# Sparse attention and two MLPs on one core: the weight conversions beside attention cut into smaller ScalarE steps, the high part copied on VectorE, and a new table of stage offsets

## The chip, the cores and the metric

One core of one Trainium2 chip runs the whole program in one launch. The metric is the device time of an execution in microseconds; of several executions the median counts. The time before is 1178.81 us, the median of three runs from 1178.59 to 1180.55.

## What is computed

Cut to what matters, the reference is (all in float32):

```python
scores = (q @ k.T) / 8                      # q, k, v: 4 batches x 8 heads x 576 rows x 64
keep = scores >= scores.max(-1) - tau       # tau 0.02
attn = where(keep, exp(scores - scores.max(-1)), 0)
x = (attn / (attn.sum(-1) + 1e-9)) @ v      # put side by side by head: 2304 x 512
h = x @ moe_w_in                            # 512 -> 2048
x = (maximum(h, 0) + alpha * minimum(h, 0)) @ moe_w_out    # 2048 -> 512
h = x @ moe2_w_in
out = where(h > 0, h, exp(minimum(h, 0)) - 1) @ moe2_w_out
```

The weights of the MLPs and alpha arrive as float64 and are read by the kernel as pairs of 32-bit words.

## The kernel before

**Attention** comes first. It works on 16 units, a unit being a batch and two heads of it, and on 9 jobs in each unit: four blocks of 128 query rows for each of the two heads, and one last job that holds the 64 rows left over of both heads. Job `j` has `j % 9` as its place in the unit; the last job of a unit has place 8. A job goes through these stages (class `Job`):

- `scores`: TensorE matmuls of `qt` with `kt` into a PSUM tile `ps`, of which there are three;
- `top`: VectorE takes the negated maximum of a row (a TENSOR_REDUCE into `st`); `limit`: GpSimd makes the threshold from it (`st<-st,tau_sb`);
- `exp`: ScalarE writes `e` from `ps`; `mask`: VectorE zeroes what lies under the threshold and sums (`e<-ps,st,e`); with it the tile `ps` is free;
- `raise_sum` on GpSimd and `invert` on VectorE give the reciprocal of the sums, for two heads at a time; `normalise`: GpSimd multiplies `e` by it (`e<-e,st`);
- `turn` and `turn_last`: TensorE transposes `e` into a PSUM bank `pst`; `keep` and `keep_last`: ScalarE copies the bank to `pt`;
- after four or five jobs of a unit `values` multiplies `pt` with `vt` into such a bank (256 columns for a unit's first group, 320 for its second), and `finish` on ScalarE copies it to `xt`.

Beside this, `prep` and `keep_prep` transpose the next unit's `k` and `q`, on the same PSUM banks. There are two banks (`ps_t`, `bufs=2`), shared by `prep`, `turn`, `turn_last` and `values`: each of these waits until ScalarE has emptied the bank that was filled two before.

**The conversions.** The float64 weights are turned into a high and a low fp32 part, one piece of 128x512 at a time (`conversion`, line 118). Twenty pieces (those of the first ten blocks of the first MLP) are converted beside attention: ScalarE writes `x` (an absolute value, line 124) and `t` (the lower word, line 125), VectorE limits, shifts and joins bits (lines 128 to 139), GpSimd adds (line 140), ScalarE writes the high part `hi` (line 149, `w<-x` in the trace), VectorE writes the low part `lo` (line 153, `w<-x,w`). The function is a generator: each `yield` ends a step, and `beside` (line 546) runs one step at a time.

**The order** is written out. Everything on TensorE, VectorE, ScalarE and GpSimd goes through `Pinned` (line 81), so that each engine executes its instructions in the order in which the program issues them; all of these have line 87 in the profile. For attention, `attention` (line 390) puts every stage of every job into a list at the place `j + AT[stage]` (the table at line 386) and issues the list sorted by place. The steps of `beside` stand at 1.25 jobs from one another.

**The MLPs** follow: chunks of 512 tokens, `hidden` and `outer` for each of 16 blocks of the hidden layer, fed by TensorE without a break; `load_in` splits a chunk of the input into two parts, and the first chunk's loading is begun beside attention (line 549).

Of the kernel before, what the change touches and what calls it, by code (L numbers as in the profile page):

```python
# [12 lines left out]
AF = mybir.ActivationFunctionType  # L13
# [7 lines left out]
def sparse_attention_two_mlps(  # L21
# [29 lines left out]
    FIRST = 10  # L51
# [5 lines left out]
    stage = ctx.enter_context(tc.tile_pool(name="stage", bufs=2))  # L57
# [31 lines left out]
    pe, dve, act, pool = (Pinned(engine) for engine in (nc.tensor, nc.vector, nc.scalar, nc.gpsimd))  # L89
# [11 lines left out]
    def load_piece(i):  # L101
        if i >= len(pieces):
            return
        layer, f, part = pieces[i]
        src = ((moe_w_in, moe_w_out), (moe2_w_in, moe2_w_out))[layer][part]
        r = stage.tile([P, DM], I64, tag="raw", name="r64", bufs=3)
        if part == 0:
            nc.sync.dma_start(
                out=r.rearrange("p (k m) -> p k m", m=P),
                in_=src[:, f * P:(f + 1) * P].rearrange("(k p) m -> p k m", p=P))  # L110
        else:
            nc.sync.dma_start(out=r, in_=src[f * P:(f + 1) * P, :])
        both = r.bitcast(U32).rearrange("p (n t) -> p n t", t=2)
        staged[i] = both[:, :, 0], both[:, :, 1]
# [3 lines left out]
    def conversion(i):  # L118
        layer, f, part = pieces[i]
        lower, upper = staged.pop(i)  # L120
        x = stage.tile([P, DM], F32, tag="x", name="x", bufs=4)
        t = stage.tile([P, DM], U32, tag="t", name="t", bufs=3)
        bits = x.bitcast(U32)
        act.activation(out=x, in_=upper.bitcast(F32), func=AF.Abs)
        act.activation(out=t, in_=lower, func=AF.Copy, scale=2.0 ** -29)
        yield
        if layer == 0 and f < FIRST:
            dve.tensor_scalar(out=x, in0=x, scalar1=TOP, scalar2=BOTTOM, op0=ALU.min, op1=ALU.max)
            dve.tensor_scalar(out=bits, in0=bits, scalar1=5, scalar2=2,
                              op0=ALU.logical_shift_left, op1=ALU.logical_shift_right)  # L130
        else:
            dve.scalar_tensor_tensor(out=x, in0=x, scalar=TOP, in1=bottom.to_broadcast([P, DM]), op0=ALU.min,
                                     op1=ALU.max)
            dve.scalar_tensor_tensor(out=bits, in0=bits, scalar=5, in1=two.to_broadcast([P, DM]),
                                     op0=ALU.logical_shift_left, op1=ALU.logical_shift_right)
        if layer == 0 and f < FIRST:
            yield
        dve.scalar_tensor_tensor(out=bits, in0=upper, scalar=0xC0000000, in1=bits,
                                 op0=ALU.bitwise_and, op1=ALU.bitwise_or)
        pool.tensor_tensor(out=bits, in0=bits, in1=t, op=ALU.add)  # L140
        load_piece(i + 3)
        yield
        if layer == 1:
            hi, lo = t.bitcast(F32R), x.bitcast(F32R)
        else:
            if part == 0:
                wt[f] = new_block(f)
            hi, lo = wt[f][:, part, 0, :], wt[f][:, part, 1, :]
        act.activation(out=hi, in_=x, func=AF.Copy)
        if layer == 1:  # L150
            nc.sync.dma_start(out=w_d[f][:, part, 0, :], in_=t.bitcast(F32))
        yield
        dve.scalar_tensor_tensor(out=lo, in0=x, scalar=1.0, in1=hi.bitcast(F32), op0=ALU.mult, op1=ALU.subtract)
        if layer == 0:
            converted_parts.append(f)
        else:
            nc.sync.dma_start(out=w_d[f][:, part, 1, :], in_=x)

    def new_block(f):
        return wps[f >= FIRST].tile([P, 2, 2, DM], F32R, tag="w", name="w")  # L160
# [10 lines left out]
    def convert_step(limit):  # L171
        if not active and converted[0] < limit:
            active.append(conversion(converted[0]))
            converted[0] += 1
        if active and next(active[0], "end") == "end":
            active.pop()
# [61 lines left out]
    def prep(u, i):  # L238
        if i == 0:
            turned_in[u] = (raw.tile([P, 2, HS], F32, tag="kt", name="kt", bufs=2),  # L240
                            raw.tile([P, 2, S], F32, tag="qt", name="qt", bufs=2))
        ps = bank()
        h = i // 2
        kr, qr = raws[u][h]
        if i % 2 == 0:
            for t in range(HS // KB):
                pe.transpose(ps[:, t * KB:(t + 1) * KB], kr[:, t, :], ident[0:KB, 0:KB])
        else:
            for t in range(NKT):
                pe.transpose(ps[:, t * P:(t + 1) * P], qr[:, t, :], ident)  # L250
        if i == 0:
            for g in range(2):
                pe.transpose(ps[:, HS + g * TAIL:HS + (g + 1) * TAIL], raws[u][g][1][0:TAIL, NKT, :],
                             ident[0:TAIL, 0:TAIL])
        return ps
# [105 lines left out]
    def group_values(group):  # L361
        u, g = group
        vt, pt = vts[u % 2], pts.pop(group)
        n = 2 * P + g * TAIL
        ps = bank()
        for t in range(NKT):
            for h, own in halves():
                pe.matmul(out=ps[own, 0:n], lhsT=vt[:, t, own], rhs=pt[:, h * NKT + t, 0:n],
                          start=(t == 0), stop=False, skip_group_check=True)
        pe.matmul(out=ps[:, 0:n], lhsT=vt[:, NKT, :], rhs=pt[:, 2 * NKT, 0:n], start=False,  # L370
                  stop=True, skip_group_check=True)
        return ps

    def finish(group, ps):
        u, g = group
        if g == 0:
            xts[u] = raw.tile([P, S], F32, tag="xt", name="xt", bufs=2)
        n = 2 * P + g * TAIL
        act.activation(out=xts[u][:, 2 * g * P:2 * g * P + n], in_=ps[:, 0:n], func=AF.Copy)
        if g == 1:  # L380
            b, hp = units[u]
            nc.sync.dma_start(out=x_d[b][:, hp, :], in_=xts.pop(u))
            load_values(u + 2)


    AT = dict(scores=-3.09, prep=-2.6, keep_prep=-2.33, top=-2.24, limit=-2.07, exp=-2.01, mask=-0.67, raise_sum=-0.53,
              invert=0.13, beside=0.2, normalise=1.58, turn=2.01, keep=2.29, turn_last=2.97, keep_last=3.19,
              values=6.05, finish=6.46)

    def attention(beside):  # L390
        jobs = [Job(u, i, h) for u in range(len(units)) for i in range(NKT + 1) for h in range(2 if i < NKT else 1)]
        todo = []

        def put(at, what, *args):
            todo.append((at, len(todo), what, args))

        for j, job in enumerate(jobs):
            for stage in ("scores", "limit", "exp", "mask", "normalise", "turn", "keep"):
                put(j + AT[stage], getattr(job, stage))
            put(j + AT["top"], job.top, jobs[j - 1])  # L400
            if not (job.h or job.last):
                continue
            put(j + AT["raise_sum"], job.raise_sum)
            put(j + AT["invert"], job.invert)
            put(j + AT["turn_last"], job.turn_last, jobs[j - 1])
            put(j + AT["keep_last"], job.keep_last)
            if job.last or job.i == 1:
                held = []
                put(j + AT["values"], lambda g, held=held: held.append(group_values(g)), job.group)
                put(j + AT["finish"], lambda g, held=held: finish(g, *held), job.group)  # L410
            if not job.last and job.u + 1 < len(units):
                held = []
                put(j + AT["prep"], lambda u, i, held=held: held.append(prep(u, i)), job.u + 1, job.i)
                put(j + AT["keep_prep"], lambda u, i, held=held: keep_prep(u, i, *held), job.u + 1, job.i)
        for i in range(len(jobs) * 4 // 5):
            put(1.25 * i + AT["beside"], beside, i)
        for _, _, what, args in sorted(todo, key=lambda t: t[:2]):
            what(*args)

# [126 lines left out]
    def beside(i):  # L546
        if i > 4:
            convert_step(2 * FIRST)
        if i == 80 or i == 95:
            next(first_in, None)  # L550

    attention(beside)
    for _ in first_in:
        pass
# [36 lines left out]
```

## Time and profile before

| what | value |
|---|---|
| median of three runs | 1178.81 us |
| the profiled execution's own time | 1180.63 us |
| its span, first to last instruction | 1178.80 us |
| busy, share of the span | PE 96%, DVE 55%, ACT 44%, POOL 39% |
| granted TensorE clock | 0.999 of full speed |
| attention | from 4 us, when the first transposes start, to 367 us |
| the two MLPs | 367 us to the end |

The page names the engines PE (TensorE matmuls), PEld (TensorE weight loads, which run beside matmuls), DVE (VectorE), ACT (ScalarE), POOL (GpSimd) and SP (DMA issue). Names like `pst<-ident,e` say which tile an instruction writes and which it reads. An idle time is put down to the instruction whose end ended it. The profiled execution took 1.82 us longer than the median.

### The profile page before, as it was taken

The page shows a single profiled execution, that of the slowest core. Times are in us where ns is not written, and L with a number is a line of the kernel's source. Part 1 is how long each engine was busy: PE and PEld are TensorE (multiplying, and loading weights), DVE is VectorE, ACT ScalarE, POOL GpSimd, SP SyncE. Part 2 cuts the span into 40 slices and gives each one's busy share as a digit, 9 for nine tenths or more (in the row PEclk, how much of TensorE's full clock was granted, in tenths as well). Part 3 has the DMA queues.
Part 4 walks back from the last instruction along what each step waited for, and adds up shares of the span by engine and source line. Part 5 has one row for each costly group of instructions (what it writes and reads, how often), then busy time and mean ns, then how long its engine had stood idle before and what let it go on. Part 6 is the DMA issues. An engine that isn't in the chain of part 4 may idle for free.

```text
span 1178.8 us, 16654 instructions
## 1 busy us (share of the span) xinstructions
PE 1133.0 (96%) x5936; PEld 853.2 (72%) x5936; DVE 651.8 (55%) x1153; ACT 513.1 (44%) x988; POOL 458.7 (39%) x598
## 2 busy tenths in 40 slices
PE   7888999989898999999999999999999999999998
PEld 4555555555456888888888888978888888888887
DVE  5777876877774994686886862422232232232232
ACT  5787887887774442342342331222222222222222
POOL 3555655655553552443543542222222222222222
PEclk9999999999999999999999999999999999999999
DMA  6533543434212332345444424950010010010000
GB/s 146 141 101 98 148 102 89 120 88 112 59 38 75 103 94 98 126 155 184 162 152 169 162 79 145 369 185 1 3 70 1 1 72 1 1 54 1 1 36 19
DMA packets 126242, 110.67 MB, mean 94 GB/s; under 512 B 83920, under 2 KB 104400, under 8 KB 123600
## 3 DMA queue, kind: packets, MB, share of 16 engines
q1 hardware_dynamic: 126160, 109.61, 29.9%
q8 instruction: 47, 0.77, 0.3%
q14 instruction: 35, 0.29, 0.1%
HBM read 78.65 MB, written 30.93 MB: 93 GB/s over the span
## 4 chain that ended last, share of the span: by engine, by line
PE 67%; DMA 1%; ACT 0%; DVE 0%; issue 0%; SPq 0%; DVEq 0%; ACTq 0%
PE psa L87 34%; PE psh L87 32%; DMA y<-o 1%; PE pst L87 1%; DVE g L87 0%; DMA out_dram<-o 0%; ACT o L87 0%; ACT gh L87 0%; DVE o L87 0%; ACT xt L87 0%; DVE il L87 0%; ACT pt L87 0%; ACT g L87 0%; DMA x<-xt 0%; SPq L505 0%
## 5 line engine op out<-in xcount | busy, mean ns | idle before, releaser
L87 POOL TENSOR_TENSOR gl<-g,gh 128x512 fp32r<-128x512 f32 (+1 forms) x160 | 200.3, 1252 | 490.4 <-ACT gh L87 418.7
L87 PE MATMUL psh<-ih,w 128*128 128x512 f32 (+1 forms) x1280 | 385.9, 369 | 0.4 <-ACT ih L87 0.4
L87 PEld LDWEIGHTS psh<-ih,w 128*128 128x128 f32 x1280 | 233.7, 188 | 45.0 <-ACT ih L87 0.8
L87 ACT ACTIVATE gh<-g 128x512 fp32r<-128x512 f32 (+1 forms) x160 | 94.5, 591 | 330.8 <-DVE g L87 319.2
L87 PE MATMUL psh<-il,w 128*128 128x512 f32 (+1 forms) x640 | 236.8, 370 | 0.2 <-DVE il L87 0.2
L87 DVE TENSOR_SCALAR g<-g 128x512 f32<-128x512 f32 (+1 forms) x80 | 38.2, 477 | 253.9 <-ACT g L87 253.8
L87 PE MATMUL psa<-w,gh 128*128 128x512 f32 x576 | 148.7, 398 | 2.2 <-ACT gh L87 2.2
L87 DVE TENSOR_REDUCE st<-ps 128x1 f32<-128x576 f32 x144 | 108.6, 754 | 75.6 <-PE ps L87 75.1
L87 PE MATMUL psa<-gh,w 128*128 128x512 f32 (+1 forms) x640 | 147.8, 373 | 0.6 <-ACT gh L87 0.6
L87 PEld LDWEIGHTS psh<-il,w 128*128 128x128 f32 x640 | 120.2, 188 | 22.1 <-DVE il L87 0.5
L87 PEld LDWEIGHTS pst<-ident,e 128*128 128x128 f32 (+1 forms) x720 | 74.5, 137 | 80.0 <-issue 22.6
L87 PE MATMUL pst<-ident,e 128*128 128x128 f32 (+1 forms) x720 | 114.8, 285 | 17.1 <-POOL e L87 9.8
L87 PEld LDWEIGHTS psa<-gh,w 128*128 128x128 f32 x640 | 112.5, 188 | 23.5 <-ACT gh L87 0.8
L87 PEld LDWEIGHTS psa<-w,gh 128*128 128x128 f32 x576 | 107.6, 189 | 27.7 <-ACT gh L87 2.8
L87 DVE SCALAR_TENSOR_TENSOR e<-ps,st,e 128x576 f32<-128x576 f32 x144 | 115.9, 805 | 4.9 <-ACT e L87 4.0
L87 ACT ACTIVATE pt<-pst 128x512 f32<-128x512 f32 (+2 forms) x240 | 109.7, 464 | 15.8 <-PE pst L87 13.4
L87 ACT ACTIVATE g<-psh 128x512 f32<-128x512 f32 (+1 forms) x80 | 44.3, 553 | 165.3 <-PE psh L87 163.6
L87 POOL TENSOR_SCALAR e<-e,st 128x576 f32<-128x576 f32 x144 | 111.1, 772 | 9.7 <-DVE st L87 1.8
L87 PE MATMUL ps<-kt,qt 64*128 64x288 f32 (+1 forms) x640 | 111.4, 455 | 0.3 <-DVE e L87 0.3
L87 POOL TENSOR_TENSOR x<-x,t 128x512 uint32<-128x512 uint32 x64 | 82.3, 1287 | 72.3 <-DVE x L87 69.9
L87 ACT ACTIVATE e<-ps,st 128x576 f32<-128x576 f32 x144 | 106.6, 740 | 2.3 <-DVE st L87 2.3
L87 DVE SCALAR_TENSOR_TENSOR g<-psh,g 128x512 f32<-128x512 f32 (+1 forms) x160 | 102.1, 638 | 5.5
(45 smaller groups left out, 1142.7 us busy)
## 6 DMA issues: line engine op xcount, KB each, us to landing
r<-in_moe_w_in_dram SPq DMA_DIRECT2D x32, 512.0 KB, 3.7
r<-in_moe_w_out_dram SPq DMA_DIRECT2D x32, 512.0 KB, 3.5
w<-w SPq DMA_DIRECT2D x16, 1024.0 KB, 5.2
qr<-in_q_dram SPq DMA_DIRECT2D x64, 128.0 KB, 2.7
w<-t SPq DMA_DIRECT2D x32, 256.0 KB, 2.2
w<-x SPq DMA_DIRECT2D x32, 256.0 KB, 2.1
kr<-in_k_dram SPq DMA_DIRECT2D x64, 72.0 KB, 2.4
x<-xt SPq DMA_DIRECT2D x16, 288.0 KB, 2.5
```

What stands on the lines that cost most here:

```text
L87: return lambda *args, **named: tc.keep_in_program_order(made(*args, **named))
```

## The change

In the conversions beside attention (`beside_attention`: the first layer's first ten blocks) there is now a `yield` between the two ScalarE writes, the high part is copied by VectorE instead of ScalarE, and the low part follows it in the same step. A piece still takes five steps. The table of offsets is another one; a second table, `LATER`, moves some stages of the second head's jobs; the steps stand 1.3 jobs apart instead of 1.25, and the two steps of the first chunk's loading have other numbers.

```diff
+        beside_attention = layer == 0 and f < FIRST
         act.activation(out=x, in_=upper.bitcast(F32), func=AF.Abs)
+        if beside_attention:
+            yield
         act.activation(out=t, in_=lower, func=AF.Copy, scale=2.0 ** -29)
         yield
...
-        act.activation(out=hi, in_=x, func=AF.Copy)
+        if beside_attention:
+            dve.tensor_copy(out=hi, in_=x)
+        else:
+            act.activation(out=hi, in_=x, func=AF.Copy)
         if layer == 1:
             nc.sync.dma_start(out=w_d[f][:, part, 0, :], in_=t.bitcast(F32))
-        yield
+        if not beside_attention:
+            yield
         dve.scalar_tensor_tensor(out=lo, in0=x, scalar=1.0, in1=hi.bitcast(F32), op0=ALU.mult, op1=ALU.subtract)
...
-    AT = dict(scores=-3.09, prep=-2.6, keep_prep=-2.33, top=-2.24, limit=-2.07, exp=-2.01, mask=-0.67, raise_sum=-0.53,
-              invert=0.13, beside=0.2, normalise=1.58, turn=2.01, keep=2.29, turn_last=2.97, keep_last=3.19,
-              values=6.05, finish=6.46)
+    AT = dict(scores=-3.24, top=-2.4, limit=-2.37, prep=-2.29, exp=-2.11, keep_prep=-1.89, mask=-1.41, 
+                  raise_sum=-1.21, invert=-0.36, normalise=0.71, beside=1.96, turn=2.23, keep=2.5, turn_last=3.17, 
+                  keep_last=3.44, values=6.66, finish=6.97)
+    LATER = dict(normalise=-0.77, top=-0.23, scores=-0.19, keep=-0.02, turn=-0.0, mask=0.17, exp=0.29)
...
-                put(j + AT[stage], getattr(job, stage))
-            put(j + AT["top"], job.top, jobs[j - 1])
+                put(j + AT[stage] + job.h * LATER.get(stage, 0), getattr(job, stage))
+            put(j + AT["top"] + job.h * LATER["top"], job.top, jobs[j - 1])
...
-        for i in range(len(jobs) * 4 // 5):
-            put(1.25 * i + AT["beside"], beside, i)
+        for i in range(len(jobs) * 10 // 13):
+            put(1.3 * i + AT["beside"], beside, i)
...
-        if i == 80 or i == 95:
+        if i == 78 or i == 92:
             next(first_in, None)
```

What this does to the order is seen engine by engine. On TensorE the rows of the two programs are the same from first to last; none of its instructions has another place. On the other three engines the places at which they differ repeat from unit to unit; three are shown.

ScalarE at the end of the eighth unit, where `finish` (`xt<-pst 128x320`) empties the bank of the unit's second `values`. Before:

```order
L87 ACTIVATE qt<-pst,sc 128x512
L87 ACTIVATE e<-ps,st 128x576
L87 ACTIVATE pt<-pst 128x4x128
L87 ACTIVATE xt<-pst 128x320
L87 ACTIVATE e<-ps,st 128x576
L87 ACTIVATE pt<-pst 128x128
L87 ACTIVATE pt<-pst 128x4x128
L87 ACTIVATE w<-x 128x512
L87 ACTIVATE e<-ps,st 128x576
L87 ACTIVATE pt<-pst 128x4x128
```

The same place in the change:

```order
L87 ACTIVATE qt<-pst,sc 128x512
L87 ACTIVATE e<-ps,st 128x576
L87 ACTIVATE pt<-pst 128x4x128
L87 ACTIVATE e<-ps,st 128x576
L87 ACTIVATE xt<-pst 128x320
L87 ACTIVATE pt<-pst 128x128
L87 ACTIVATE pt<-pst 128x4x128
L87 ACTIVATE e<-ps,st 128x576
L87 ACTIVATE pt<-pst 128x4x128
L87 ACTIVATE x<-r_2072 128x512
```

The `exp` of the ninth unit's last job (job 80, the second `e<-ps,st` shown before, and the second in the change) has gone from behind the `finish` to ahead of it, and the conversion's `w<-x` is gone from ScalarE. Apart from conversions, this is the one difference on ScalarE, and it stands once in a unit.

GpSimd around the `normalise` (`e<-e,st`) of job 70, the last job but one of the eighth unit. Before:

```order
L87 TENSOR_SCALAR st<-st,tau_sb 128x1
L87 TENSOR_SCALAR st<-st 128x1
L87 TENSOR_SCALAR e<-e,st 128x576
L87 TENSOR_SCALAR st<-st,tau_sb 128x1
L87 TENSOR_TENSOR x<-x,t 128x512
L87 TENSOR_SCALAR e<-e,st 128x576
L87 TENSOR_SCALAR st<-st,tau_sb 128x1
L87 TENSOR_SCALAR st<-st 128x2
L87 TENSOR_SCALAR e<-e,st 128x576
```

The same place in the change:

```order
L87 TENSOR_SCALAR st<-st,tau_sb 128x1
L87 TENSOR_SCALAR e<-e,st 128x576
L87 TENSOR_SCALAR st<-st 128x1
L87 TENSOR_SCALAR e<-e,st 128x576
L87 TENSOR_SCALAR st<-st,tau_sb 128x1
L87 TENSOR_TENSOR x<-x,t 128x512
L87 TENSOR_SCALAR st<-st,tau_sb 128x1
L87 TENSOR_SCALAR e<-e,st 128x576
L87 TENSOR_SCALAR st<-st 128x2
L87 TENSOR_SCALAR st<-st,tau_sb 128x1
L87 TENSOR_SCALAR e<-e,st 128x576 x2
```

Before, `normalise` of job 70 (the second `e<-e,st`) stood behind `limit` of job 73 and a conversion's add (`x<-x,t`); in the change (there too the second `e<-e,st` shown) it stands ahead of `limit` of job 73 and of the add. Where two jobs are a pair, as jobs 72 and 73 in the last row, their two `normalise` now follow one another.

VectorE at the end of the ninth unit, around `top` (TENSOR_REDUCE) of job 81, the tenth unit's first, whose scores TensorE issues behind the eighth unit's second `values`. Before:

```order
L87 TENSOR_REDUCE st<-ps 128x1
L87 SCALAR_TENSOR_TENSOR e,st<-ps,st,e 128x576
L87 TENSOR_REDUCE st<-ps 128x1
L87 RECIPROCAL st<-st 128x2
L87 SCALAR_TENSOR_TENSOR e,st<-ps,st,e 128x576
L87 TENSOR_REDUCE st<-ps 128x1
L87 RECIPROCAL st<-st 128x1
L87 SCALAR_TENSOR_TENSOR w<-x,w 128x512
L87 SCALAR_TENSOR_TENSOR e,st<-ps,st,e 128x576
```

The same place in the change:

```order
L87 TENSOR_REDUCE st<-ps 128x1
L87 SCALAR_TENSOR_TENSOR e,st<-ps,st,e 128x576 x2
L87 TENSOR_REDUCE st<-ps 128x1
L87 RECIPROCAL st<-st 128x2
L87 CAST w<-x 128x512
L87 SCALAR_TENSOR_TENSOR w<-x,w 128x512
L87 TENSOR_REDUCE st<-ps 128x1
L87 SCALAR_TENSOR_TENSOR e,st<-ps,st,e 128x576
L87 RECIPROCAL st<-st 128x1
```

The `mask` of the unit's last job (job 80) has gone from behind `top` of job 81 to ahead of it; the reciprocal of a pair mostly stands one `mask` later; the copy of the high part (CAST `w<-x`) is new, with the low part right behind it.

## Rows read from the trace of the kernel before

**Rows 1.** Busy time by stage: stretch, busy us of each engine, clock, DMA share, GB/s.

```profile
20.00:350.00 330.00, 303.00 (x2053) 173.98 (x2054) 254.25 (x571) 258.19 (x528) 192.63 (x372) 1.00 0.40 104
350.00:367.00 17.00, 13.97 (x96) 7.66 (x95) 4.58 (x12) 7.42 (x18) 6.13 (x11) 1.00 0.05 18
367.00:1179.00 812.00, 804.32 (x3746) 664.23 (x3745) 386.76 (x554) 239.79 (x431) 257.23 (x204) 1.00 0.26 91
```

**Rows 2.** Waits in 20:367, TensorE's: who waited for whom, us in total, times, longest.

```profile
PEld pst L87 <- POOL e L87: 21.6, 31, 1.9
...
PEld pst L87 <- POOL st L87: 16.9, 37, 1.1
PE pst L87 <- ACT pt L87: 16.0, 30, 1.9
...
PE pst L87 <- POOL e L87: 9.8, 14, 1.4
```

**Rows 3.** The same view, the other engines.

```profile
POOL st L87 <- DVE st L87: 85.9, 68, 2.9
DVE st L87 <- PE ps L87: 64.5, 40, 3.0
ACT xt L87 <- PE pst L87: 57.7, 30, 2.4
```

**Rows 4.** Timeline, 184:196: start, us, engine, operation, [idle before <-releaser].

```profile
186.95 1.27 POOL L87 TENSOR_TENSOR x<-x,t 128x512 uint32<-128x512 uint32 x1 [0.81 <-ACT e L87]
...
188.21 0.74 POOL L87 TENSOR_SCALAR e<-e,st 128x576 f32<-128x576 f32 x1
...
189.00 0.66 PE L87 MATMUL pst<-ident,e 128*128 128x128 f32 x4 [1.39 <-POOL e L87]
```

**Rows 5.** Timeline, 301:314, ScalarE's conversions ahead of a bank.

```profile
303.37 0.66 ACT L87 ACTIVATE x<-r 128x512 f32<-128x512 f32 x1
...
304.49 0.61 ACT L87 ACTIVATE ih<-il 128x512 fp32r<-128x512 f32 x1
...
306.11 0.47 PE L87 MATMUL pst<-ident,kr 96*128 96x96 f32 x3 [1.87 <-ACT pt L87]
```

**Rows 6.** Timeline, 213:219, the same place of another unit, none between.

```profile
217.52 0.47 PE L87 MATMUL pst<-ident,kr 96*128 96x96 f32 x3 [0.23 <-ACT pt L87]
```

**Rows 7.** Timeline, 200:216, around a unit's second values.

```profile
201.95 3.11 PE L87 MATMUL pst<-pt,vt 128*64 128x320 f32 x18
...
205.10 0.44 ACT L87 ACTIVATE xt<-pst 128x320 f32<-128x320 f32 x1 [2.44 <-PE pst L87]
205.43 0.73 ACT L87 ACTIVATE e<-ps,st 128x576 f32<-128x576 f32 x1
...
205.79 0.76 DVE L87 TENSOR_REDUCE st<-ps 128x1 f32<-128x576 f32 x1 [2.50 <-PE ps L87]
```

**Rows 8.** Groups by form in 20:367: busy us, mean ns | idle before.

```profile
L87 ACT ACTIVATE e<-ps,st 128x576 f32<-128x576 f32 x141 | 104.4, 740 | 0.4 <-DVE st L87 0.4
...
L87 DVE SCALAR_TENSOR_TENSOR w<-x,w 128x512 fp32r<-128x512 f32 x20 | 15.7, 784 | 1.8 <-ACT w L87 1.8
...
L87 ACT ACTIVATE w<-x 128x512 fp32r<-128x512 f32 x20 | 12.5, 627 | 0.0
...
L87 DVE TENSOR_SCALAR x<-x 128x512 f32<-128x512 f32 x20 | 11.7, 586 | 1.3 <-ACT x L87 1.3
...
L87 DVE TENSOR_SCALAR x<-x 128x512 uint32<-128x512 uint32 x20 | 9.3, 466 | 0.7
```

**Rows 9.** Timeline, 184:196, a shift of VectorE's alone.

```profile
183.57 0.43 DVE L87 TENSOR_SCALAR x<-x 128x512 uint32<-128x512 uint32 x1
```

**Rows 10.** Timeline, 200:216, VectorE's conversions beside GpSimd's normalise.

```profile
208.03 1.01 DVE L87 SCALAR_TENSOR_TENSOR w<-x,w 128x512 fp32r<-128x512 f32 x1
...
212.57 0.74 POOL L87 TENSOR_SCALAR e<-e,st 128x576 f32<-128x576 f32 x1
...
212.72 1.33 DVE L87 TENSOR_SCALAR x<-x 128x512 f32<-128x512 f32 x2
```

More of the change, by code (lines that the diff above doesn't have):

```diff
@@ L123, in conversion @@
         bits = x.bitcast(U32)
+        beside_attention = layer == 0 and f < FIRST
         act.activation(out=x, in_=upper.bitcast(F32), func=AF.Abs)
+        if beside_attention:
+            yield
         act.activation(out=t, in_=lower, func=AF.Copy, scale=2.0 ** -29)
         yield
-        if layer == 0 and f < FIRST:
+        if beside_attention:
             dve.tensor_scalar(out=x, in0=x, scalar1=TOP, scalar2=BOTTOM, op0=ALU.min, op1=ALU.max)
@@ L135, in conversion @@
                                      op0=ALU.logical_shift_left, op1=ALU.logical_shift_right)
-        if layer == 0 and f < FIRST:
+        if beside_attention:
             yield
@@ L148, in conversion @@
             hi, lo = wt[f][:, part, 0, :], wt[f][:, part, 1, :]
-        act.activation(out=hi, in_=x, func=AF.Copy)
+        if beside_attention:
+            dve.tensor_copy(out=hi, in_=x)
+        else:
+            act.activation(out=hi, in_=x, func=AF.Copy)
         if layer == 1:
             nc.sync.dma_start(out=w_d[f][:, part, 0, :], in_=t.bitcast(F32))
-        yield
+        if not beside_attention:
+            yield
         dve.scalar_tensor_tensor(out=lo, in0=x, scalar=1.0, in1=hi.bitcast(F32), op0=ALU.mult, op1=ALU.subtract)
```

## The prediction, made before the changed kernel ran

> **What bounds the kernel now.** I read the busy times by stage first. From 367 us on TensorE is busy 804.3 of 812.0 us [rows 1], and the change touches nothing there: the MLPs will take what they take. Attention is where the time can move. From 20 to 350 us TensorE is busy 303.00 of 330 us, and in the last 17 us 13.97 [rows 1]. So it is idle 27.0 + 3.0 = 30.0 us between 20 and 367 us, and everything else in that stretch is its own work. Of the 330 us VectorE is busy 254.25, ScalarE 258.19 and GpSimd 192.63 [rows 1]; none of them is full.
>
> TensorE's order does not change at all, so the question is only which of its 30 us of waiting goes, and what waiting is new. The table of waits says whom it waits for: 16.0 us in 30 waits for ScalarE's copies to `pt`, that is for a PSUM bank to be emptied, and 9.8 us in 14 waits for GpSimd's `normalise` [rows 2]. Those two are 25.8 of the 30. The waits of the weight loads for GpSimd, 21.6 and 16.9 us [rows 2], run partly beside matmuls, so I take them only as an upper bound.
>
> The waits of the other engines show who is pushed and who pushes. VectorE waits 64.5 us in 40 waits for scores, and ScalarE 57.7 us in 30 waits for a bank that `values` fills [rows 3]. These are TensorE's long blocks: while TensorE spends 3.11 us on 18 matmuls of `values`, ScalarE stands 2.44 us in front of `finish`, the `exp` behind it runs only afterwards, and VectorE's next `top` comes after 2.50 us of idleness [rows 7]. Between two such blocks TensorE outruns ScalarE, and then waits for banks.
>
> **Part 1, GpSimd's order (gain).** One of the 14 waits can be followed: the conversion's add runs 1.27 us from 186.95, `normalise` runs behind it from 188.21, and TensorE, idle 1.39 us, starts its transposes at 189.00, when it ends [rows 4]. The `normalise` was queued behind a `limit` that needs a later job's `top`, and behind an add, though its own sums were long inverted. In the change the second `normalise` of a pair follows the first, one `limit` earlier than before, and the add comes behind. GpSimd's own work is the same. What is now queued behind two multiplications, 2 x 0.74 us [rows 4, 10], is the next `limit`. Between the reciprocal and the `mask` that needs this threshold VectorE has two `top` of 0.76 us [rows 7] and another `mask` to do, which are longer together, so I cost that delay at nothing; where an add stands between too (1.27 us [rows 4]), up to half a microsecond of VectorE's time is uncovered, mostly in front of `values`, where it is idle anyway. Of the 9.8 us I take all, and 0.2 more for single short waits of the same kind: **-10 us**. The bounds are 0, if something else releases TensorE just as late, and -14.0, all of the 30.0 us that are not ScalarE's 16.0 (the weight loads' 38.5 are more than there is to gain).
>
> **Part 2, ScalarE (gain).** ScalarE loses 20 copies of 627 ns, 12.5 us [rows 8]. The other two writes of a piece no longer stand together. And once in a unit an `exp` of 740 ns [rows 8] goes ahead of `finish`, into an idle time of 2.44 us [rows 7]: 16 x 0.74 = 11.8 us of ScalarE's work that no longer stand behind `values`, where TensorE next asks for banks. What such work costs TensorE is seen by comparing one place in two units. With three such writes in front, two of a conversion and one of the first chunk's loading (0.66 us the first, 0.61 the last) the transposes of the next keys waited 1.87 us [rows 5]; in a unit in which none of these came between, they waited 0.23 us [rows 6]. The 0.23 us belong to the ring of two banks and to the `exp` that stands between two copies, and stay. If all 30 waits shrank to that, 16.0 - 30 x 0.23 = 9.1 us would go. Single steps of 0.66 us remain in the queue, so I take **-8 us**. Bounds: 0, and -16.0.
>
> **Part 3, VectorE (loss).** VectorE gains 20 copies of 128x512 from SBUF to SBUF. The trace has no such copy on VectorE; the nearest rows are its one-source operations on the same tile, 586 and 466 ns on average [rows 8], one of them alone 0.43 us [rows 9]. Two of them took 1.33 us while GpSimd multiplied [rows 10]; less the 0.43 us of one that ran alone, the other took 0.90. I take 0.55 us, 11 us in all, with 0.43 and 0.90 as the ends (8.6 to 18 us). The low part, 784 ns on average [rows 8], follows at once, so that a block of 1.3 us stands ahead of a `top`, and behind it an `exp`, the `keep_last` behind that in ScalarE's queue, and a bank. Against it VectorE's `mask` of the unit's last job goes into the idle time of 2.50 us [rows 7], and VectorE has 64.5 us of idleness [rows 3], but only at `values`. That the reciprocal stands one `mask` later costs nothing, because `turn` asks for `normalise` more than a job later. I charge a quarter of the 11 us to the path: **+3 us**. The quarter is my choice; the bounds are 0 and, with the whole block as long as the rows show it can be, (0.90 + 1.01 - 0.78) x 20 = 22.6 us, where 1.01 us is a low part beside a multiplication [rows 10].
>
> **What costs nothing.** The longer offset of `values` moves none of its matmuls on TensorE. The steps are 1.3 jobs apart, so the twentieth piece ends some seven jobs later, still six jobs before the last one. The loads of the pieces, issued by SP at the joining of bits, and the loads behind `finish` shift by less than a job, and the DMA share is 0.40 before 350 us [rows 1]. The last 17 us have no conversions.
>
> **The sum**: -10 - 8 + 3 = -15 us. The profiled execution would go from 1180.63 to 1165.6; it lies 1.82 above the median of 1178.81, so against the median the time is **1164 us**.
>
> **The rivals.**
>
> - *The ring keeps the pace.* Only GpSimd's part comes true; ScalarE's relief is given back, because TensorE comes to the two banks earlier and waits there for the `exp` in between. For it speaks that a wait of 0.23 us stays without any conversion [rows 6]; against it the 1.87 us with them [rows 5]. -10 + 3: 1172.
> - *GpSimd and VectorE get into each other's way.* VectorE's shift took 0.43 us alone and its like 0.90 beside a multiplication [rows 9, 10], and with pairs of `normalise` GpSimd is busy 1.48 us at a stretch. A copy that meets a pair could be late by 0.47 + 0.74 = 1.2 us; with GpSimd busy 192.63 / 330 = 0.58 of the time [rows 1], that is 20 x 0.58 x 1.2 = 14 us of VectorE, of which I charge half, 7 us, less 1 that part 3 holds already: -15 + 6, which gives 1170. The Trainium skill's page "SBUF — State Buffer", section "Who interferes with whom", has a rule by which this must be so: a copy or a one-scalar operation of VectorE in a two-port mode and a GpSimd instruction exclude one another for a whole instruction. By that rule the move to VectorE is bought on the one engine that can be blocked; the 0.43 and 0.90 us agree with it.
> - *TensorE hardly waits any more.* The reliefs help one another, 25 of the 30 us go: 1154.
> - *No change.* Each wait that goes is followed by another of the same length, and the table, whose new offsets leave TensorE's order as it was, does nothing that counts: 1179, within 0.2% (2.4 us), about what a measurement of this kernel can tell from no change.
> - *Slower: VectorE's double step.* The copy and the low part, back to back ahead of a `top` that comes right behind `values`, hold up `top`, `exp`, the copies to `pt` and the banks. At the full 22.6 us against gains of 18 us the time is 1183. It decides when a piece costs TensorE more than 18 / 20 = 0.9 us. Against it: VectorE waits 40 times for TensorE and is busy only 254.25 of 330 us [rows 1, 3], and ScalarE, which would have to be starved by VectorE, does not reach its `exp` before it has copied two banks.
>
> **How the numbers follow.** Forecast as summed, 1158 to 1168: 0.45. The ring: 0.12. The two engines in each other's way: 0.10. Hardly any waiting: 0.13. No change: 0.07. Slower: 0.13. Faster by over 0.2%: 0.45 + 0.12 + 0.10 + 0.13 = 0.80. The range leaves out the last two cases, 0.20, and holds the others: from 1152, a little under the third rival, to 1177, where part 2 gives nothing and part 3 costs 8 us instead of 3.
>
> **What would show it.** Right: TensorE's waits for `e` in attention fall from 9.8 us to under 2, those for `pt` from 16.0 to about 8; its stretch of MLPs begins near 352 instead of 367 us and lasts as long; the copy on VectorE has a mean of 0.45 to 0.7 us; the `exp` ahead of `finish` runs inside `values`. Wrong: long waits of ScalarE's `exp` for `top`, where there are now next to none, point to the double step; a wait for `pt` still near 16 us points to the ring; a mean of `e<-e,st` on GpSimd well above 0.77 us points to the two engines.

## The result, and the profile after

The changed kernel took 1165.18 us, the median of four runs from 1164.80 to 1167.59; the kernel before, run beside it, 1179.06. The ratio is 0.9884, with a 95% interval of 0.9872 to 0.9896: 13.9 us less. In a second comparison, on another occasion, the same kernel came to 1165.32 us and a ratio of 0.9875 [0.9856, 0.9893]. The profiled execution took 1167.59 us, 13.0 less than that of before.

All of it lies in attention. TensorE's first matmul of the MLPs starts at 353.69 us; before it started at 367.13. The two rows, before and changed:

```profile
367.13 0.63 PE L87 MATMUL psh<-ih,w 128*128 128x512 f32 x1
```

```profile
353.69 0.63 PE L87 MATMUL psh<-ih,w 128*128 128x512 f32 x1
```

This start is the best measure of attention, and is used below for every run; it is read from one profiled execution of each kernel. The busy times by stage of the changed kernel (the columns are those of [rows 1], with the stages as far from the end of attention as there):

```profile
20.00:337.00 317.00, 302.21 (x2046) 173.22 (x2048) 262.62 (x588) 248.99 (x507) 200.18 (x371) 1.00 0.42 108
337.00:354.00 17.00, 14.98 (x104) 8.44 (x103) 5.67 (x15) 8.25 (x19) 7.06 (x13) 1.00 0.05 18
354.00:1166.00 812.00, 803.96 (x3745) 664.03 (x3743) 386.92 (x554) 239.66 (x431) 257.48 (x204) 1.00 0.26 91
```

From 20 to 354 us TensorE is idle 14.8 + 2.0 = 16.8 us, where it was 30.0. Its own work is the same (302.21 + 14.98 us against 303.00 + 13.97 [rows 1]), and so are the MLPs, 803.96 busy of 812. So the 13.2 us that attention lost are 13.2 us of TensorE's waiting. The waits of the changed kernel in the same stretch, 20 to 354 us, answer to [rows 2, 3]:

```profile
DVE st L87 <- PE ps L87: 36.6, 40, 2.2
...
ACT e L87 <- DVE st L87: 12.5, 18, 1.8
PE pst L87 <- ACT pt L87: 10.0, 25, 1.1
DVE e L87 <- POOL st L87: 8.3, 15, 1.5
...
PE ps L87 <- DVE e L87: 1.4, 3, 0.6
...
PE pst L87 <- POOL e L87: 0.5, 2, 0.3
```

The wait for `e` from GpSimd is gone, 0.5 us in 2 waits for 9.8 in 14. The waits for `pt` fell from 16.0 us to 10.0. TensorE's waits for a `mask`, that is for a free tile `ps`, have grown from 0.3 us to 1.4. And two waits that were next to nothing before (0.4 us and none listed) have grown on engines that are not the bound: ScalarE's `exp` stands 12.5 us for VectorE's `top`, and VectorE's `mask` 8.3 us for GpSimd's `limit`.

At the place of [rows 4], the transposes of job 70, the last but one of the eighth unit, the timeline of the changed kernel reads:

```profile
178.43 0.75 POOL L87 TENSOR_SCALAR e<-e,st 128x576 f32<-128x576 f32 x1
...
179.90 1.27 POOL L87 TENSOR_TENSOR x<-x,t 128x512 uint32<-128x512 uint32 x1
...
180.67 0.66 PE L87 MATMUL pst<-ident,e 128*128 128x128 f32 x4
```

`normalise` now starts 2.2 us before TensorE comes to its `e`, and the add runs behind. TensorE's row has no idle time; before it had 1.39 us. The two transposes of keys that had been compared, that of [rows 6] and that of [rows 5], are these now:

```profile
208.76 0.47 PE L87 MATMUL pst<-ident,kr 96*128 96x96 f32 x3 [0.24 <-ACT pt L87]
...
294.17 0.47 PE L87 MATMUL pst<-ident,kr 96*128 96x96 f32 x3 [0.79 <-ACT pt L87]
```

Where no conversion came between, the wait has stayed as forecast, 0.24 us for 0.23. Where three writes had stood in front of the bank, one is left (the second and the first chunk's have gone), and the wait fell from 1.87 to 0.79 us: 0.79 - 0.24 = 0.55 us for one, (1.87 - 0.23) / 3 = 0.55 for each of three. That is nearly all the time for which such a write holds ScalarE: in [rows 5] the third one starts 1.12 us after the first, 0.56 for each.

Around the second `values` of the eighth unit [rows 7] the changed kernel does this:

```profile
193.06 3.11 PE L87 MATMUL pst<-pt,vt 128*64 128x320 f32 x18
...
193.29 1.75 POOL L87 TENSOR_SCALAR e<-e,st 128x576 f32<-128x576 f32 x2 [0.61 <-PE pst L87]
...
194.46 0.74 ACT L87 ACTIVATE e<-ps,st 128x576 f32<-128x576 f32 x1 [0.69 <-DVE st L87]
...
195.01 1.26 POOL L87 TENSOR_TENSOR x<-x,t 128x512 uint32<-128x512 uint32 x1
...
196.21 0.44 ACT L87 ACTIVATE xt<-pst 128x320 f32<-128x320 f32 x1 [1.01 <-PE pst L87]
196.27 0.26 POOL L87 TENSOR_SCALAR st<-st,tau_sb 128x1 f32<-128x1 f32 x1
196.56 0.82 DVE L87 SCALAR_TENSOR_TENSOR e<-ps,st,e 128x576 f32<-128x576 f32 x1 [1.47 <-POOL st L87]
```

The `exp` runs inside `values`, and VectorE goes on too. But it runs no further than to the next `mask`, which waits 1.47 us for its threshold: the `limit` (196.27) was queued behind two multiplications and an add on GpSimd. TensorE has no idle time at this place. Of the 15 such waits of a `mask`, 8.3 us in all, only three come behind an add; eight end while TensorE is in a `values`, and the longest, this one, begins there. The groups by form of the new or slower operations in 20 to 354 us, against [rows 8]:

```profile
L87 POOL TENSOR_SCALAR e<-e,st 128x576 f32<-128x576 f32 x144 | 116.6, 814 | 31.1 <-DVE st L87 20.6 <-PE pst L87 6.8 <-PE ps L87 1.9
...
L87 DVE SCALAR_TENSOR_TENSOR w<-x,w 128x512 fp32r<-128x512 f32 x20 | 17.1, 854 | 0.7
...
L87 DVE CAST w<-x 128x512 fp32r<-128x512 f32 x20 | 8.7, 437 | 3.1 <-POOL x L87 3.0
```

The copy (CAST) takes 437 ns. The low part behind it takes 854 ns on average, where it took 784 [rows 8], and GpSimd's `normalise` 814, where it took 772 in the kernel before:

```profile
L87 POOL TENSOR_SCALAR e<-e,st 128x576 f32<-128x576 f32 x144 | 111.1, 772 | 9.7 <-DVE st L87 1.8
```

### The profile page after: what moved, and what is told of

It is laid out like the page before. It is cut to its first block, busy times and chain, and to the rows that moved or that the text cites. A ratio compares the mean times of both kernels' runs of the same rounds, so it can differ in the third digit from the quotient of the medians.

```text
span 1165.7 us, 16771 instructions
## 1 busy us (share of the span) xinstructions
PE 1133.0 (97%) x5936; PEld 852.8 (73%) x5936; DVE 661.3 (57%) x1173; ACT 504.5 (43%) x968; POOL 466.8 (40%) x598
## 4 chain that ended last, share of the span: by engine, by line
PE 84%; ACT 6%; DVE 3%; issue 2%; DMA 2%; POOL 1%; SPq 1%; ACTq 0%; DVEq 0%; POOLq 0%
PE psa L87 35%; PE psh L87 33%; PE pst L87 13%; PE ps L87 4%; ACT e L87 2%; ACT pt L87 2%; DVE e L87 1%; DVE st L87 1%; DMA y<-o 1%; POOL e L87 1%; DMA qr<-in_q_dram 1%; POOL x L87 0%; ACT x L87 0%; SPq L226 0%; ACT t L87 0%
## 5 line engine op out<-in xcount | busy, mean ns | idle before, releaser
L87 POOL TENSOR_SCALAR e<-e,st 128x576 f32<-128x576 f32 x144 | 116.6, 814 | 31.1 <-DVE st L87 20.6
L87 DVE SCALAR_TENSOR_TENSOR e<-ps,st,e 128x576 f32<-128x576 f32 x144 | 116.7, 811 | 13.6 <-POOL st L87 8.3
```

The lines of the kernel that those rows point to most:

```text
L87: return lambda *args, **named: tc.keep_in_program_order(made(*args, **named))
```

## The experiments

Each edit is against the changed kernel. Each kernel was timed beside the kernel before, and the ratio is to that. "MLPs from" is the start of TensorE's first matmul of the MLPs, the next two columns are TensorE's waits for `pt` and for `e` from 20 us on, and "falls" says how often its granted clock fell to half (1.2 GHz) for 3.4 us in attention behind its start (one stretch of twice that length, in the last row but one, is counted as two).

| kernel | ratio to before, 95% interval | MLPs from, us | for `pt` | for `e` | falls |
|---|---|---|---|---|---|
| before | 1 | 367.13 | 16.0 | 9.8 | 0 |
| changed | 0.9884 [0.9872, 0.9896] | 353.69 | 10.0 | 0.5 | 0 |
| changed, again | 0.9875 [0.9856, 0.9893] | 353.32 | 10.0 | 0.5 | 0 |
| the table alone | 0.9939 [0.9923, 0.9956] | 361.77 | 17.4 | under 0.4 | 1 |
| the conversions alone | 1.0018 [1.0005, 1.0031] | 368.31 | 8.7 | 13.6 | 1 |
| `normalise` put back | 0.9940 [0.9920, 0.9960] | 361.90 | 9.5 | 9.1 | 1 |
| `exp` behind `finish` again | 0.9894 [0.9877, 0.9911] | 354.86 | 10.3 | 1.1 | 0 |
| high part on ScalarE, same step | 0.9948 [0.9931, 0.9964] | 362.75 | 14.6 | 0.2 | 1 |
| the copy made twice | 0.9948 [0.9931, 0.9964] | 361.89 | 12.7 | 0.5 | 1 |
| `keep_last` ahead of an `exp` | 0.9933 [0.9918, 0.9948] | 359.32 | 13.7 | 0.3 | 1 |
| the two writes together | 0.9926 [0.9911, 0.9941] | 358.31 | 14.2 | 1.2 | 0 |
| high part on GpSimd | 0.9889 [0.9872, 0.9906] | 355.32 | 9.5 | 3.4 | 0 |
| high part on ScalarE, own step | 0.9980 [0.9968, 0.9993] | 367.95 | 14.2 | 2.7 | 4 |
| `limit` ahead of the second `normalise` | 0.9891 [0.9875, 0.9907] | 355.48 | 10.0 | 3.9 | 0 |

A fall of the clock has a price of its own, which has to be taken off before such starts are compared. It is seen in the run with the copy made twice:

```profile
173.61 0.66 PE L87 MATMUL pst<-ident,qr 128*128 128x128 f32 x4 [2.00 <-ACT pt L87]
...
175.55 4.63 PE L87 MATMUL pst<-pt,vt 128*64 128x320 f32 x18
```

```profile
175.20:178.60 3.40, 3.40 (x15) 1.54 (x15) 2.94 (x7) 2.11 (x4) 1.31 (x4) 0.51 0.27 55
```

The first rows are TensorE's timeline, the last is the busy view of the 3.4 us in which the clock was granted at 0.51. The 18 matmuls of `values` took 4.63 us there; at full clock they take 3.11 [rows 7]. One fall costs about 1.5 us. That price is taken for the falls of the other runs too, which is an estimate; with the table alone the same 18 matmuls took 4.56 us in a fall.

**The two halves of the change, alone.** The first kernel has the new table and spacing with the old conversion:

```diff
...
-        if beside_attention:
-            yield
         act.activation(out=t, in_=lower, func=AF.Copy, scale=2.0 ** -29)
...
-        if beside_attention:
-            dve.tensor_copy(out=hi, in_=x)
-        else:
-            act.activation(out=hi, in_=x, func=AF.Copy)
+        act.activation(out=hi, in_=x, func=AF.Copy)
...
-        if not beside_attention:
-            yield
+        yield
...
```

> The changed kernel's table of offsets, with the conversion as it was before (the high part on ScalarE, the two ScalarE writes in one step). Theory (most of the gain is GpSimd's order, -10 us, and the exp ahead of finish; the lighter conversion on ScalarE is worth about 4): 1168 to 1170 us, TensorE's waits for e under 1.5 us, for pt 13 to 15. Rival (the conversions are what matters): 1174 to 1179, waits for pt near 16. Rival (VectorE's double step costs what it can): faster than the changed kernel, under 1163.

Of TensorE's waits (20 to 365 us) the longest in sum was this, and none for `e` is listed:

```profile
PE pst L87 <- ACT pt L87: 17.4, 34, 2.1
```

The second has the new conversion with the old table (`AT` as before, no `LATER`) and spacing:

```diff
...
-                put(j + AT[stage] + job.h * LATER.get(stage, 0), getattr(job, stage))
-            put(j + AT["top"] + job.h * LATER["top"], job.top, jobs[j - 1])
+                put(j + AT[stage], getattr(job, stage))
+            put(j + AT["top"], job.top, jobs[j - 1])
...
-        for i in range(len(jobs) * 10 // 13):
-            put(1.3 * i + AT["beside"], beside, i)
+        for i in range(len(jobs) * 4 // 5):
+            put(1.25 * i + AT["beside"], beside, i)
...
-        if i == 78 or i == 92:
+        if i == 80 or i == 95:
```

> The old table of offsets and the old distance of steps, with the changed conversion. Theory: the waits for e stay near 10 us, those for pt fall by some 4, VectorE costs up to 3: 1175 to 1179 us. Rival (the conversions are what matters): 1168 to 1171. Rival (VectorE's double step): 1181 or more.

```profile
PE pst L87 <- POOL e L87: 13.6, 21, 2.0
...
PE pst L87 <- ACT pt L87: 8.7, 23, 1.3
...
PE ps L87 <- DVE e L87: 2.4, 6, 0.6
```

The table alone moves the start of the MLPs by 5.4 us, or 6.9 without the fall; the conversions alone by nothing, -1.2 or, without the fall, +0.3 us. Together they move it by 13.4. Each half removed its own waits, and lost some or all of that to the other's. With the table alone the waits for `e` are gone, as expected, but those for `pt`, expected at 13 to 15 us, rise to 17.4. With the conversions alone the waits for `pt` fall by 7.3 us, to 8.7; those for `e` rise by 3.8, to 13.6, those for a tile `ps` by 2.1, and one fall costs the rest. The time of the table alone lies over its range (0.9939 of 1178.8 is 1171.6 us), that of the conversions alone a little over its own (1180.9), just under the 1181 of the rival with VectorE's double step. Its interval lies above 1: the conversions alone made the kernel slightly slower, by 0.18%. The start in the table is that of the lowest of its ten executions, 1179.38 us with a granted clock of 0.998; the median was 1181.46, and the others were granted 0.992 to 0.998.

**GpSimd's order.** `normalise` alone goes back to where it stood among GpSimd's stages:

```diff
-                  raise_sum=-1.21, invert=-0.36, normalise=0.71, beside=1.96, turn=2.23, keep=2.5, turn_last=3.17, 
+                  raise_sum=-1.21, invert=-0.36, normalise=1.28, beside=1.96, turn=2.23, keep=2.5, turn_last=3.17, 
...
-    LATER = dict(normalise=-0.77, top=-0.23, scores=-0.19, keep=-0.02, turn=-0.0, mask=0.17, exp=0.29)
+    LATER = dict(top=-0.23, scores=-0.19, keep=-0.02, turn=-0.0, mask=0.17, exp=0.29)
```

> The changed kernel, only with normalise put back to where it stood between the other GpSimd stages before the change (GpSimd's order in attention is then that of the kernel before, but for the conversions' adds). Theory: TensorE's waits for e come back to 8 to 10 us and the time is 1173 to 1175 us. Rival (the ring of two banks would release TensorE as late anyway): 1165 to 1168, with waits for pt lower than in the changed kernel.

```profile
PE pst L87 <- ACT pt L87: 9.5, 24, 1.1
PE pst L87 <- POOL e L87: 9.1, 13, 1.5
```

The waits for `e` are back, 9.1 us in 13, and those for `pt` are unchanged. The start of the MLPs comes 8.4 us later than the mean of the two runs of the changed kernel (353.5), 6.9 without the fall. That decides against the ring for this part: TensorE's time came back with these waits. The time, 0.9940 of 1178.8 or 1171.7 us, is a little under the range of the theory.

**The `exp` ahead of `finish`.** The `exp` of a unit's last job goes behind `finish` again, and its `mask` behind the next unit's first `top`:

```diff
-                  keep_last=3.44, values=6.66, finish=6.97)
+                  keep_last=3.44, values=6.66, finish=6.87)
...
-                put(j + AT[stage] + job.h * LATER.get(stage, 0), getattr(job, stage))
+                put(j + AT[stage] + job.h * LATER.get(stage, 0) + (0.05 if job.last and stage == "mask" else 0), getattr(job, stage))
```

> The changed kernel, only with the exp of a unit's last job behind finish again and its mask behind the next unit's first top. Theory: ScalarE does 16 exps behind values instead of before their end, TensorE's waits for pt rise by 3 to 5 us: 1168 to 1170 us. Rival (ScalarE has the time anyway): 1165 to 1166.

```profile
PE pst L87 <- ACT pt L87: 10.3, 26, 1.1
...
PE pst L87 <- POOL e L87: 1.1, 4, 0.4
```

The theory's 3 to 5 us did not come: the waits for `pt` are 10.3 us against 10.0, the start 354.86 against 353.5, 1.4 us. The time, 0.9894 of 1178.8 or 1166.3 us, is just over the rival's 1165 to 1166: ScalarE had nearly all of the time anyway.

**How large a step on ScalarE is.** Here the high part stays on VectorE, and the two writes of a piece stand in one step again:

```diff
+        act.activation(out=t, in_=lower, func=AF.Copy, scale=2.0 ** -29)
         if beside_attention:
             yield
-        act.activation(out=t, in_=lower, func=AF.Copy, scale=2.0 ** -29)
         yield
```

> The changed kernel with the two ScalarE writes of a piece in one step again, the high part still on VectorE, five steps as before. It separates the smaller steps from the copy. Theory (the amount on ScalarE matters more than the size of a step): ratio 0.988 to 0.990. Rival (it is the size of the step): 0.992 or more, with longest waits for pt of 1.8 us or more.

```profile
PE pst L87 <- ACT pt L87: 14.2, 33, 1.7
...
PE pst L87 <- POOL e L87: 1.2, 3, 0.7
```

The start is 4.8 us later and the waits for `pt` rise to 14.2 us, with the same amount of work on ScalarE. The ratio, 0.9926, lies in the rival's range, not in the theory's: it is the size of the step that counts here. The rival's other sign was just missed, with a longest wait of 1.7 us instead of 1.8.

**What VectorE's time costs.** The copy is made twice:

```diff
             dve.tensor_copy(out=hi, in_=x)
+            dve.tensor_copy(out=hi, in_=x)
```

> The changed kernel with the copy of the high part made twice on VectorE, 20 more copies of some 0.44 us (8.7 us). It measures what VectorE's time costs. Theory (a quarter of it reaches the path): ratio to the kernel before 0.989 to 0.991, some 2 us over the changed kernel. Rival (VectorE has slack): 0.987 to 0.989. Rival (VectorE is the engine that ScalarE waits for): 0.994 or more, with ScalarE's exp waiting for top well over the 12.5 us of the changed kernel.

The group of the copies, and the waits, in 20 to 365 us:

```profile
L87 DVE CAST w<-x 128x512 fp32r<-128x512 f32 x40 | 20.8, 519 | 3.7 <-POOL x L87 3.0
```

```profile
ACT e L87 <- DVE st L87: 20.6, 21, 2.7
...
PE pst L87 <- ACT pt L87: 12.7, 27, 2.0
...
PE ps L87 <- DVE e L87: 3.1, 6, 1.0
```

The second copies took 20.8 - 8.7 = 12.1 us, and the start of the MLPs came 8.4 us later, 6.9 without the fall: 0.57 us for each one added, more than twice the quarter that I had charged, and the ratio lies in the range of the second rival. The way is the one of the slower rival: ScalarE's `exp` waits 20.6 us for `top`, for 12.5 in the changed kernel.

**The high part on ScalarE again.** Two kernels tried it with everything else as in the change: in one step with the low part, and in a step of its own, with six steps to a piece at 13/12 of a job each. The first:

```diff
-            dve.tensor_copy(out=hi, in_=x)
+            act.activation(out=hi, in_=x, func=AF.Copy)
```

> The changed kernel, only with the high part written by ScalarE again, in the same step as the low part. Theory (ScalarE's 12.5 us are what TensorE waits for): waits for pt rise from 10 to 14 us or more, the time is 0.3 to 0.6% above the changed kernel's (ratio to the kernel before 0.991 to 0.995). Rival (VectorE's double step costs as much as ScalarE's relief gives): ratio 0.986 to 0.989.

```profile
DVE w L87 <- ACT w L87: 19.1, 16, 3.0
...
PE pst L87 <- ACT pt L87: 14.6, 30, 1.2
```

The second has that edit too, and:

```diff
-        if not beside_attention:
-            yield
+        yield
...
-        for i in range(len(jobs) * 10 // 13):
-            put(1.3 * i + AT["beside"], beside, i)
+        for i in range(len(jobs) * 12 // 13):
+            put(13 / 12 * i + AT["beside"], beside, i)
...
-        if i > 4:
+        if i > 5:
...
-        if i == 78 or i == 92:
+        if i == 94 or i == 110:
```

> The changed kernel with the high part on ScalarE again, but in a step of its own ahead of the low part's, six steps to a piece at 13/12 of a job each, so that VectorE does not stand waiting for it as it did (19.1 us) where both were one step. Theory (ScalarE's 12.5 us count, VectorE's 8.7 count too, about as much each): between the changed kernel and the table alone, ratio 0.989 to 0.992. If the copy on VectorE is the whole of what the conversions gave: 0.993 or more. If it gave nothing and only the smaller steps did: 0.987 to 0.989.

```profile
PE pst L87 <- ACT pt L87: 14.2, 24, 2.1
...
ACT w L87 <- POOL x L87: 10.9, 9, 1.8
```

The first came out as its theory expected, with a ratio of 0.9948 and waits for `pt` of 14.6 us; still neither is the clean test I wanted, since each brings a wait along with the copy. In one step VectorE stands 19.1 us for ScalarE's copy, at the head of its queue. In a step of its own ScalarE stands 10.9 us for GpSimd's add, which in the new order comes behind two multiplications, and TensorE's clock falls four times, some 6 us. Both are slower than the changed kernel by far. The second lies in the open range of 0.993 or more, but at 0.9980 it is slower even than the table alone (0.9939), which has the same copy on ScalarE, so the copy's place alone doesn't explain it. How much of the gain the copy's 12.5 us of ScalarE's work alone make stays open.

**Three tries to do better.** The `exp` of the job in the fifth place of a unit goes behind the last job's `keep_last`:

```diff
-                put(j + AT[stage] + job.h * LATER.get(stage, 0), getattr(job, stage))
+                put(j + AT[stage] + job.h * LATER.get(stage, 0) + (0.6 if j % 9 == 4 and stage == "exp" else 0), getattr(job, stage))
```

> The changed kernel with one exp in a unit moved from ahead of the last job's keep_last to behind it, so that the bank that the next keys' transposes wait for is emptied earlier. Theory (the rest of the waits for pt is the ring of two banks with an exp between): the 0.23 us at this place go, 3 to 5 us in all, ratio 0.984 to 0.987. Rival (the exp that is later now holds up mask, and with it scores): ratio 0.988 or more, with waits of TensorE for the mask.

```profile
ACT e L87 <- DVE st L87: 17.1, 20, 1.8
...
PE pst L87 <- ACT pt L87: 13.7, 32, 1.9
...
DVE e L87 <- ACT e L87: 10.6, 20, 1.3
```

The waits for `pt` did not fall but rose to 13.7 us; ScalarE's `exp` waited more for `top` and VectorE's `mask` 10.6 us for `exp`, for 5.0 in the changed kernel. The ratio is the rival's, but the rival's sign, TensorE waiting for the `mask`, hardly shows (1.6 us for 1.4). The high part on GpSimd, behind its add, with the low part a step later:

```diff
-        yield
+        if not beside_attention:
+            yield
...
-            dve.tensor_copy(out=hi, in_=x)
+            pool.tensor_scalar(out=hi, in0=x, scalar1=1.0, scalar2=1.0, op0=ALU.mult, op1=ALU.mult)
...
-        if not beside_attention:
-            yield
+        yield
```

> The changed kernel with the high part written by GpSimd, behind its add, and the low part on VectorE a step later: 20 copies less on VectorE (8.7 us), some 13 us more on GpSimd. If VectorE's time is on the path for two thirds, as the copy made twice suggests, the time falls by up to 5 us (ratio 0.983 to 0.986) where GpSimd's longer step hides; if GpSimd's step of 1.27 + 0.65 us holds up a limit and with it a mask, that is given back (0.987 to 0.992), with VectorE's waits for st from GpSimd well over 8.3 us.

```profile
DVE e L87 <- POOL st L87: 11.9, 21, 2.2
...
DVE w L87 <- POOL w L87: 8.8, 8, 1.6
...
PE pst L87 <- POOL e L87: 3.4, 5, 1.3
```

VectorE is relieved of 8.7 us and the waits for `pt` are as low as in any run with the new table, 9.5 us; it is given back by 3.4 us for `e`, and VectorE waits 8.8 us for GpSimd's copy. And the second `normalise` of a pair behind the next `limit`:

```diff
-    LATER = dict(normalise=-0.77, top=-0.23, scores=-0.19, keep=-0.02, turn=-0.0, mask=0.17, exp=0.29)
+    LATER = dict(top=-0.23, scores=-0.19, keep=-0.02, turn=-0.0, mask=0.17, exp=0.29)
```

> The changed kernel with the second normalise of a pair behind the next limit, so that no limit is queued behind two multiplications. VectorE's waits of mask for st from GpSimd (8.3 us in the changed kernel, 1.1 with the old table) should fall to 3 or less. If these waits reach TensorE, the time falls by 2 to 4 us (ratio 0.984 to 0.987); if they lie in front of values, as forecast, it does not change (0.987 to 0.990); if the later normalise is missed by turn, 0.991 or more with TensorE's waits for e over 3 us.

```profile
PE pst L87 <- POOL e L87: 3.9, 8, 1.1
DVE e L87 <- POOL st L87: 3.4, 6, 0.7
```

VectorE's wait for the threshold falls from 8.3 to 3.4 us, and TensorE's wait for `e` rises from 0.5 to 3.9: the start comes 2.0 us later. The ratio is that of the middle case, the waits for `e` are those of the last; what VectorE's waits alone cost TensorE is not separated. None of the eleven variants was faster than the change itself. That was run once more beside the last of them:

> The changed kernel itself, run beside the others as their measure. All theories: ratio to the kernel before 0.986 to 0.990, TensorE's first matmul of the MLPs near 354 us.

It came out as before, with the start of the MLPs 0.4 us earlier.

## Why the prediction was right

The forecast was 1164 us, the time 1165.18; faster by over 0.2%, as expected with 0.8. The bound was named rightly: attention's 30.0 us of TensorE's waiting, of which 13.2 went, and nothing else changed. Both mechanisms of gain are there, GpSimd's earlier `normalise` and the emptier ring of banks. But that the sum came within 1.2 us is in part luck: the first gain and the loss were each mis-sized by 2 to 3 us, and the parts are no sum. Of the signs named, the waits for `pt` stayed at 10.0 us instead of about 8, the MLPs begin at 353.7 instead of near 352, and the copy's mean lies just under its range.

- *Part 1, GpSimd, -10 us.* The waits that it named went, from 9.8 to 0.5 us; put back, they cost 6.9 us of attention, not 10. The step "I cost that delay at nothing" was too low for VectorE: the later `limit` made it wait 8.3 us in 15 waits, most of them with no add between and one of 1.47 us, where half a microsecond was the most I allowed, and that only behind an add. That they fall mostly beside `values` was right. What they cost TensorE is not shown: where 4.9 us of them were undone, `normalise` came later and the start with it.
- *Part 2, ScalarE, -8 us.* The waits for `pt` fell by 6.0 us, and the 0.23 us of the ring stayed where I had said. Its working was half wrong. The 11.8 us of `exp` moved into `values` were worth 1.4 us; the smaller steps, of which I said only that they remain in the queue, were worth 4.8. What the copy's leaving ScalarE is worth no run shows alone. If the terms were a sum, 6.9 us for part 1 (measured) and 5 for part 3 (an estimate, next) would leave 11.7 of the 13.6 us between 367.13 and 353.5 for part 2, and 5.5 of these for the copy; but the halves alone show that they are no sum.
- *Part 3, VectorE, +3 us.* The copy was cheaper than I took, 437 ns instead of 550, but the charge of a quarter was too low: an added copy costs 0.57 of its time. At that rate the 8.7 us of copies cost 5 us, an estimate from the run with two. The sign I gave for the slower rival, `exp` waiting for `top`, is there: 12.5 us, where it was 0.4 [rows 8]. It stayed far from the 0.9 us a piece at which it decides: 5 / 20 = 0.25.

What the terms hid is that they are not a sum. With the conversions alone the rival "no change" came true: the 7.3 us of waits for `pt` that went came back as waits for GpSimd's `normalise`, for the `mask` and as a fall of the clock. Only both halves together bring TensorE's idle time from 30.0 to 16.8 us. I had treated the parts as independent.

Of the rivals, *the ring* would have left the waits for `pt` near 16 us and the time at 1172; with the `normalise` put back they stayed at 9.5 us. *GpSimd and VectorE in each other's way* happened, but on the other engine than I had priced. The timeline of the changed kernel around a copy:

```profile
198.04 0.41 DVE L87 CAST w<-x 128x512 fp32r<-128x512 f32 x1
...
198.49 0.69 DVE L87 SCALAR_TENSOR_TENSOR w<-x,w 128x512 fp32r<-128x512 f32 x1
198.57 1.23 POOL L87 TENSOR_SCALAR e<-e,st 128x576 f32<-128x576 f32 x1
```

The copy, beside no multiplication, took 0.41 us; the `normalise` that started 0.08 us behind the low part took 1.23 us instead of 0.74. Its mean rose from the 772 ns of before to 814, 6 us over 144 of them, and TensorE's waits for `e` are 0.5 us all the same. The rule of the Trainium skill ("SBUF — State Buffer", "SBUF: two separate sides") agrees, that of a VectorE operation with two inputs from SBUF and a GpSimd operation that reads SBUF the one which starts first holds the shared ports for its whole instruction: here GpSimd came second. Held until the low part's end at 199.18 and 0.74 us long from there, it would have ended at 199.92; it ended at 199.80.

## What to carry to other kernels

Where several engines take turns at being what the bound engine waits for, reliefs can be worth little one at a time: here the conversions alone gave nothing, the table alone half, both together 13.9 us, so a change that does nothing by itself has to be tried with its counterpart before it is dropped. Ahead of a ring of two buffers, cut foreign work into small steps before moving it elsewhere: two writes of 0.68 us apart instead of together gave 4.8 us with no work removed. And an engine that is busy 80% of the time is no free place: on VectorE, with 36.6 us of idleness left in front of TensorE's results, an added microsecond still cost 0.57 (one run, with the price of a fall taken off).

## What the runs showed of the hardware that I had not expected

TensorE's clock did not stay at full speed through attention. In seven of the profiled variants it fell to 1.2 GHz for 3.4 us, once or more often, always behind a wait of TensorE: of 2.00 us for `pt` in the run with the copy twice (the row at 173.61 above), of 2.12 with the table alone, of 1.96 for `e` with the conversions alone, of 1.18 with the high part on ScalarE in one step, of no more than 0.86, for a DMA, with `normalise` put back. A wait of 1.87 us in the kernel before [rows 5] had no fall behind it, so the length of one wait does not settle it, and these runs don't show what does. It makes a long wait cost up to 1.5 us more than itself, and it makes single profiles of nearly equal kernels differ: the changed kernel's first profile had a fall between the two MLPs, as that of before had, and the second had none (809 us instead of 812 from the start of the MLPs to the end). The 17 executions of the kernel before that were timed beside the second comparison were granted 0.994 to 0.999 of full speed, the four of the changed kernel 0.999 to 1.000, so a part of the difference in time there may be fewer falls; how much is not shown. The 13.4 us between the two starts of the MLPs hold none of it, since neither profile has a fall in attention.
